# Decode attention with a gate: K turned in 32x32 blocks on VectorE, block-diagonal queries, longer K/V chunks and a ring of 3

## The chip, the cores and the metric

The kernel runs on one core of one Trainium2 chip. The metric is the device time of one execution in microseconds; less is better. All times are medians of several executions. PE is TensorE, PEld its weight loads, DVE is VectorE, ACT is ScalarE, POOL is GpSimd, SP is the queue that issues the large loads. The "span" is the time of the profiled execution on the core; it is about 2 us less than the device time.

## The reference, cut to what matters

```
q = (x @ wq) -> 16 heads of 256          # one token
k_cache, v_cache: [8 groups, 65536 keys, 256] bf16     # 2 heads share a group
p = softmax(q . k / 16);  o = p . v;  a = o @ wo       # 448 outputs
b = small MLP on layernorm(x)
out = g * a + (1 - g) * b,  g = sigmoid(sum(x * gate_w))
```

K and V are 2 x 268 MB, and each element is used for two heads only. The kernel has to read 537 MB and does little with them.

## The kernel before

K and V of one group come in chunks of 64 rows per partition: 32 KB per partition, 4 MB per load. Each chunk is 4 steps of 16 rows per partition. Loads go into a ring of 5 slots, K and V in turn. The matmul needs K with the head dimension on the partitions, so K is turned. Before the change PE turns it (16 transposes per step, two bf16 values taken as one fp32), and DVE copies the result from PSUM:

```python
NB = 64; SB = 16; STEPS = NB // SB; RING = 5; LAG = 4
...
def transposes(n, half):
    ...
    for jj in range(8):
        nc.tensor.transpose(tp[:, 128 * jj:128 * jj + 128], kn[:, j0 + jj, :], ident[:])
    nc.vector.tensor_copy(
        out=kT[n % 2][:, 8 * DH * half:8 * DH * (half + 1)], in_=tp[:].bitcast(BF16)
    )

def scores(n):               # four column groups of PE side by side, 8 matmuls of 512 columns
    for c in range(2):
        for a in range(4):
            nc.tensor.matmul(sc[n % 2][32 * a:32 * a + 32, :], lhsT=qT[:, c, g]..., 
                rhs=kv[:, :, 32 * a:32 * a + 32, c], ..., tile_position=(0, 32 * a))
    nc.scalar.activation(out=p_t[n % 2][:], in_=sc[n % 2][:], func=ACT.Exp, ...)

def p_transpose(n):
    nc.vector.transpose(out=pT_t[n % NPT][:], in_=p_t[n % 2][:])
# p_v(n - LAG): 8 matmuls with V;  per step 32 matmuls and 32 weight loads on PE
# at the end of a group: o_scale (DVE), o_turn (PE), o_out (PE)
```

The softmax here doesn't subtract the row's maximum and nothing guards it: scores larger than these inputs give would overflow.

## Time and profile before

Time before: 1289.4 us, median of 3 runs (1289.29 to 1289.5).

| of the span of 1287.6 us | value | view |
|---|---|---|
| PE busy | 74% | busy table |
| DVE busy | 62% | busy table |
| DMA, 20 to 1250 us | share 1.00, about 430 GB/s | table by stretches |
| period of one K and V pair | 19.66 us | landings in the chain of waits |
| last V rows in, end of the span | 1279.9 us, 1287.6 us | DMA packets in the trace, page |

First, lines of the page of the kernel before: the slices (share of the DMA engines in tenths, and their rate), the DMA queues with packets, MB and share, and the chain that ended last by engine.

```profile
DMA  9999999999999999999999999999999999999995
GB/s 392 431 430 433 427 432 425 429 432 429 433 425 433 429 431 428 429 430 429 432 429 426 433 430 430 430 430 427 435 427 433 425 430 431 430 430 418 436 421 241
...
q1 hardware_dynamic: 19730, 540.55, 98.0%
...
q8 instruction: 66, 1.08, 0.3%
...
DMA 62%; PE 37%; DVE 1%; issue 0%; ACT 0%; SPq 0%; ACTq 0%; DVEq 0%
```

The DMA is full in every slice but the last. Queue 8 has 66 packets of 16 KB. The trace has 8454 matmuls and 8454 weight loads; 66 times 256 is 16,896, so these are PE's instructions, 256 to a packet (16,908 were recorded).

Second, the table by stretches of the kernel before: stretch and its length, busy time of the engines (instructions), granted PE clock, DMA share, GB/s.

```profile
1200.00:1240.00 40.00, 30.96 (x274) 19.02 (x273) 25.51 (x27) 5.56 (x17) 0.00 (x0) 0.87 1.00 428
...
1260.00:1270.00 10.00, 10.00 (x103) 6.42 (x103) 9.45 (x10) 2.67 (x8) 0.00 (x0) 1.00 0.96 396
1270.00:1275.00 5.00, 5.00 (x56) 3.04 (x57) 4.63 (x6) 0.74 (x3) 0.00 (x0) 1.00 0.57 236
1275.00:1280.00 5.00, 3.62 (x49) 1.55 (x48) 3.99 (x6) 1.38 (x4) 0.00 (x0) 1.00 0.37 145
```

Third, groups of instructions before: line, engine, operation, output and input with shapes, count, busy us and mean ns, and the idle time before them.

```profile
L316 DVE COPY kT_141<-tps_75 128x2048 bf16<-128x2048 bf16 x128 | 156.4, 1222 | 95.2 <-PE tps_75 L315 94.8
L337 DVE STREAM_TRANSPOSE pT_145<-p_143 128x512 bf16<-128x512 bf16 x43 | 30.2, 701 | 0.0
```

### The profile page before, as it was taken

The page shows a single profiled execution, that of the slowest core. Times are in us where ns is not written, and L with a number is a line of the kernel's source. Part 1 is how long each engine was busy: PE and PEld are TensorE (multiplying, and loading weights), DVE is VectorE, ACT ScalarE, POOL GpSimd, SP SyncE. Part 2 cuts the span into 40 slices and gives each one's busy share as a digit, 9 for nine tenths or more (in the row PEclk, how much of TensorE's full clock was granted, in tenths as well). Part 3 has the DMA queues.
Part 4 walks back from the last instruction along what each step waited for, and adds up shares of the span by engine and source line. Part 5 has one row for each costly group of instructions (what it writes and reads, how often), then busy time and mean ns, then how long its engine had stood idle before and what let it go on. Part 6 is the DMA issues. An engine that isn't in the chain of part 4 may idle for free.

```text
span 1287.6 us, 19500 instructions
## 1 busy us (share of the span) xinstructions
PE 952.5 (74%) x8454; PEld 595.9 (46%) x8454; DVE 792.6 (62%) x859; ACT 193.2 (15%) x543; POOL 80.2 (6%) x101
## 2 busy tenths in 40 slices
PE   4586777876877767778768677696786876877878
PEld 3354444544544444445445444454454544544544
DVE  3565755756666557566566575674665755656657
ACT  0111111211111111111111111111111111111111
POOL 2110111100111001110000000000000000000000
PEclk9887888888888788788888897887887888889889
DMA  9999999999999999999999999999999999999995
GB/s 392 431 430 433 427 432 425 429 432 429 433 425 433 429 431 428 429 430 429 432 429 426 433 430 430 430 430 427 435 427 433 425 430 431 430 430 418 436 421 241
DMA packets 21196, 545.49 MB, mean 424 GB/s; under 512 B 2675, under 2 KB 2806, under 8 KB 3958
## 3 DMA queue, kind: packets, MB, share of 16 engines
q1 hardware_dynamic: 19730, 540.55, 98.0%
q0 software_dynamic: 1376, 3.69, 0.8%
q8 instruction: 66, 1.08, 0.3%
q14 instruction: 20, 0.16, 0.0%
q10 hardware_dynamic: 4, 0.00, 0.0%
HBM read 544.22 MB, written 0.00 MB: 423 GB/s over the span
## 4 chain that ended last, share of the span: by engine, by line
DMA 62%; PE 37%; DVE 1%; issue 0%; ACT 0%; SPq 0%; ACTq 0%; DVEq 0%
DMA ring_73<-in_A_k_cache_dram 15%; PE tps_74 L315 12%; DMA ring_69<-in_A_k_cache_dram 12%; DMA ring_72<-in_A_k_cache_dram 12%; PE tps_75 L315 12%; DMA ring_71<-in_A_k_cache_dram 12%; DMA ring_70<-in_A_k_cache_dram 11%; PE pv L347 6%; PE sc_77 L325 4%; PE sc_76 L325 3%; DMA ring_73<-in_A_wq_dram 1%; PE misc L292 0%; PE misc L247 0%; DVE kT_142 L316 0%; PE misc L357 0%
## 5 line engine op out<-in xcount | busy, mean ns | idle before, releaser
L316 DVE COPY kT_141<-tps_74 128x2048 bf16<-128x2048 bf16 x128 | 154.8, 1209 | 350.5 <-PE tps_74 L315 350.5
L316 DVE COPY kT_141<-tps_75 128x2048 bf16<-128x2048 bf16 x128 | 156.4, 1222 | 95.2 <-PE tps_75 L315 94.8
L331 ACT ACTIVATE p_144<-sc_77 128x512 bf16<-128x512 f32 x128 | 76.4, 597 | 710.0 <-PE sc_77 L325 710.0
L316 DVE COPY kT_142<-tps_75 128x2048 bf16<-128x2048 bf16 x128 | 156.7, 1224 | 25.2 <-PE tps_75 L315 24.6
L316 DVE COPY kT_142<-tps_74 128x2048 bf16<-128x2048 bf16 x128 | 152.7, 1193 | 7.8 <-PE tps_74 L315 7.3
L331 ACT ACTIVATE p_143<-sc_76 128x512 bf16<-128x512 f32 x128 | 76.4, 597 | 368.8 <-PE sc_76 L325 368.8
L315 PE MATMUL tps_74<-ident,ring_69 128*128 128x128 f32 x416 | 68.7, 318 | 66.6 <-DMA ring_69<-in_A_k_cache_dram 66.5
L315 PE MATMUL tps_74<-ident,ring_71 128*128 128x128 f32 x416 | 68.8, 319 | 65.5 <-DMA ring_71<-in_A_k_cache_dram 65.5
L315 PE MATMUL tps_74<-ident,ring_70 128*128 128x128 f32 x416 | 66.0, 310 | 63.5 <-DMA ring_70<-in_A_k_cache_dram 63.5
L315 PE MATMUL tps_74<-ident,ring_73 128*128 128x128 f32 x416 | 67.0, 313 | 58.5 <-DMA ring_73<-in_A_k_cache_dram 58.0
L315 PE MATMUL tps_74<-ident,ring_72 128*128 128x128 f32 x384 | 62.3, 315 | 63.8 <-DMA ring_72<-in_A_k_cache_dram 63.8
L325 PE MATMUL sc_77<-kT_142,qT 128*32 128x512 bf16 x1024 | 105.0, 495 | 1.2 <-DVE kT_142 L316 1.2
L315 PEld LDWEIGHTS tps_74<-ident,ring_71 128*128 128x128 f32 x416 | 54.6, 163 | 91.5 <-issue 89.4
L315 PEld LDWEIGHTS tps_74<-ident,ring_69 128*128 128x128 f32 x416 | 54.8, 163 | 89.6 <-issue 88.0
L315 PEld LDWEIGHTS tps_74<-ident,ring_70 128*128 128x128 f32 x416 | 52.3, 158 | 86.6 <-issue 84.9
L315 PEld LDWEIGHTS tps_74<-ident,ring_73 128*128 128x128 f32 x416 | 53.1, 160 | 82.4 <-issue 77.6
L315 PEld LDWEIGHTS tps_74<-ident,ring_72 128*128 128x128 f32 x384 | 49.3, 161 | 85.3 <-issue 83.6
L325 PE MATMUL sc_76<-kT_141,qT 128*32 128x512 bf16 x1024 | 79.3, 385 | 0.2
L315 PE MATMUL tps_75<-ident,ring_69 128*128 128x128 f32 x416 | 67.8, 316 | 0.0
L315 PE MATMUL tps_75<-ident,ring_71 128*128 128x128 f32 x416 | 66.7, 312 | 0.0
L315 PEld LDWEIGHTS tps_75<-ident,ring_69 128*128 128x128 f32 x416 | 53.8, 161 | 26.9 <-issue 26.9
L315 PEld LDWEIGHTS tps_75<-ident,ring_71 128*128 128x128 f32 x416 | 52.8, 159 | 27.6 <-issue 27.6
(133 smaller groups left out, 976.5 us busy)
## 6 DMA issues: line engine op xcount, KB each, us to landing
ring_69<-in_A_k_cache_dram SPq DMA_DIRECT2D x13, 4096.0 KB, 25.1
ring_70<-in_A_v_cache_dram SPq DMA_DIRECT2D x13, 4096.0 KB, 34.5
ring_71<-in_A_k_cache_dram SPq DMA_DIRECT2D x13, 4096.0 KB, 24.8
ring_72<-in_A_v_cache_dram SPq DMA_DIRECT2D x13, 4096.0 KB, 34.2
ring_73<-in_A_k_cache_dram SPq DMA_DIRECT2D x13, 4096.0 KB, 24.5
ring_69<-in_A_v_cache_dram SPq DMA_DIRECT2D x13, 4096.0 KB, 33.9
ring_70<-in_A_k_cache_dram SPq DMA_DIRECT2D x12, 4096.0 KB, 24.2
ring_71<-in_A_v_cache_dram SPq DMA_DIRECT2D x12, 4096.0 KB, 33.6
```

What stands on the lines that cost most here:

```text
L315: nc.tensor.transpose(tp[:, 128 * jj:128 * jj + 128], kn[:, j0 + jj, :], ident[:])
L316: nc.vector.tensor_copy(out=kT[n % 2][:, 8 * DH * half:8 * DH * (half + 1)], in_=tp[:].bitcast(BF16))
L325: nc.tensor.matmul(sc[n % 2][32 * a:32 * a + 32, :], lhsT=qT[:, c, g].rearrange("p r x -> p (r x)"), rhs=kv[:, :, 32 * a:32 * a + 32, c], ...
L331: nc.scalar.activation(out=p_t[n % 2][:], in_=sc[n % 2][:], func=ACT.Exp, scale=scale, accum_out=den[g % 2][:, n % steps_g:n % steps_g + 1],)
L347: nc.tensor.matmul(pv[32 * a:32 * a + 4, :], lhsT=pT[:, i, :, 0], rhs=vt[:, j * DH:(j + 2) * DH], start=first and i < 4, stop=last and i > ...
```

## The change

The intent is to take the turning of K off PE, to halve PE's instructions, to have one softmax per chunk instead of one per step, and to make rows longer. DVE turns K in 32x32 blocks. A 32x32 transpose does not gather a whole head dimension, so the queries are laid out block-diagonally: with 8 full-width matmuls per step, a window that slides by one column per step puts each step's scores on other rows of one PSUM tile. The chunks are of 6, 6, 5, 5, 5 and 5 steps (48 or 40 KB per partition) in a ring of 3. The diff, cut to its core:

```diff
-NB = 64
-STEPS = NB // SB
-RING = 5
-LAG = 4
+SIZES = (6, 6, 5, 5, 5, 5)
+RING = 3
+PAD = MAXS - 1
+WIN = 128 + PAD
...
-    def transposes(n, half):
-        ... 16 PE transposes per step, 2 copies from PSUM
+    def turn(i, s, n):
+        kn = ring[2 * i % RING][:].bitcast(FP32)
+        nc.vector.transpose(
+            out=kT[n % 2][:].bitcast(FP32), in_=kn[:, s * SB * 128:(s + 1) * SB * 128]
+        )
...
+        for q in range(8):
+            nc.tensor.matmul(
+                sc[i % 2][:], lhsT=qw[g % 2][:, q, PAD - s:PAD - s + 128], rhs=kv[:, :, q // 2, :, q % 2],
+                start=(s == 0 and q == 0), stop=(s == sizes[c] - 1 and q == 7),
+            )
...
+    for i in range(total):          # per chunk: all turns and scores, one softmax, all P V
+        for s in range(sizes[c]):
+            turn(i, s, n); scores(i, s, n); ...
+        load(2 * i + RING)
+        softmax(i)
+        for s in range(sizes[c]): p_v(i, s)
+        load(2 * i + 1 + RING)
```

## The prediction

> **What bounds the kernel now: the DMA engines, not compute.** The page's slices show DMA 9 in every slice but the last, at 425 to 433 GB/s. The Trainium skill ("DMA: Bandwidth & Descriptors", "Where 436 GB/s comes from") puts the ceiling of the ports at 435.2 GB/s; this trace comes within 1.5%. The table by stretches shows a DMA share of 1.00 from 20 to 1250 us. The chain of waits is 62% DMA: each pair of K and V takes 19.66 us (landings at 539.1, 578.5 and 617.8 us for every second pair), and PE works about 15 us of it, then idles 4 to 6 us. Loads are issued some 5 us before the one ahead lands (24 us from issue to landing, 19.7 us per pair), so the queue never runs dry. PE 74%, DVE 62% are not binding. Only the end is serial: the last data lands near 1279.8, the end is 1287.6; 6 us of it is normalise, turn, project.
>
> **What the change removes.** 16 fp32 PE transposes per step (2.05 us warm for 16) and two PSUM copies (1.2 us each); the exp and the P transpose per step (0.6 + 0.19 and 0.70 us) become one per chunk. All off the critical path.
>
> **What it adds.** One VectorE block transpose per step, 128x2048 fp32. The bf16 one of 128x512 takes 701 ns, about 0.17 us plus one column per cycle. The skill's "Vector Engine (DVE) Microarchitecture Reference" (3.8) says one element per cycle per lane, and this trace agrees for bf16; no 4-byte one is here. Estimate 2.3 us per step, 590 us in all. Scores become 8 full-width 512-column matmuls one after another instead of four column groups side by side (0.55 us for 8, so about 0.27 us each): about 2.1 us per step, 550 us. Estimates: DVE about 640 us (50%), PE about 700 us (55%). A 6-step chunk needs about 14 us of turning and 18 us to its softmax, against 29.5 us in which its 48 KB of K and of V arrive. With three slots, V of the next chunk is issued some 15 us after K lands, K after that at about 22 us; each time one load is still whole in the queue. The DMA stays saturated: the ring of 3 costs nothing in the steady part.
>
> **What moves the time.**
> 1. Rows of 40 or 48 KB instead of 32 KB. In the trace's packets 32 KB took 1215 ns and 8 KB 311 ns: 9.7 ns fixed per packet. A quarter of the packets go: about -2.5 us.
> 2. Half of PE's instructions go; each 16 KB instruction fetch lengthened one neighbouring K/V packet by about 0.5 us, on one of some eight engines in turn (66 fetches): about -2 us.
> 3. The end: V is ready earlier, no PE backlog: about -1 us.
> 4. The last K's pieces are issued only after the K before it is turned (5 steps, about 12.7 us with a cold PE), while the one load in flight lasts 12.3 us: a hole of about 1.5 us: +1.5 us.
>
> Sum: about -4 us: **1285 us, range 1277 to 1292.** Faster by over 2%: 0.02; within 2%: 0.94; slower: 0.04.
>
> **Signs.** Right: DMA still 9 in all slices and about 430 GB/s; block transposes near 2.3 us; PE and DVE shares falling to 50 to 60%; DMA over 60% of the chain. A hole in DMA near 1240 to 1260 us shows point 4.
>
> **What would make it wrong.** The 4-byte transpose taking two cycles per element (4.5 us): a 6-step chunk then takes 27 us of 29.5, slots come free too late, and the time could pass 1300. Long rows split into smaller packets: no gain in 1. Full-array matmuls throttled to half speed (3.4 us per step) would lengthen the hole.

## The result, and the profile after

After the change: 1283.0 us (1281.83 to 1283.69, 4 runs), against 1289.35 us before (4 runs). The ratio is 0.995, 95% interval 0.9933 to 0.9967. Ratios are the mean time of one kernel's runs over that of the other's of the same rounds, so not quite the ratio of the medians quoted. The forecast of 1285 us and its range held, in part by luck. As the terms below show, the fetch term was too small by 3.5 to 4.2 us and a hole of 1.5 us did not come; the end term, wrong in its sign, and the row term together took back 2.0 to 2.7 us of that.

The same lines of the page as before, for the kernel after:

```profile
DMA  9999999999999999999999999999999999999996
GB/s 395 435 426 431 434 434 431 425 433 434 430 422 434 430 429 432 424 431 432 430 436 414 432 437 434 427 421 430 435 429 438 419 430 429 436 430 419 439 420 288
...
q1 hardware_dynamic: 15410, 540.55, 98.4%
...
q8 instruction: 34, 0.56, 0.2%
...
DMA 56%; PE 24%; DVE 14%; issue 6%; ACT 1%; DVEq 0%; SPq 0%
```

It is still a kernel bound by DMA. PE has fallen to 60% and DVE to 51%, as expected; that this alone is worth nothing is shown by the run e9 below. The instruction packets went from 66 to 34.

The groups that cost most after the change:

```profile
L351 DVE STREAM_TRANSPOSE kT_265<-ring_71 128x2048 f32<-128x2048 f32 x48 | 110.2, 2295 | 74.8 <-DMA ring_71<-in_A_k_cache_dram 63.3
...
L359 PE MATMUL sc_72<-kT_265,qw_283 128*128 128x512 bf16 x288 | 93.6, 481 | 113.7 <-DVE kT_265 L351 113.7
```

The block transpose of 128x2048 fp32 takes 2295 ns, as estimated. The trace after also has one of 128x128 fp32, with 311 ns. The two give 1.03 ns per column and 0.18 us fixed, and with these a transpose of 512 columns should take 0.71 us; the bf16 ones took 711 ns. So 4-byte elements go at the same rate per column as 2-byte ones. The trace of before has one size only and could not show this split.

The end of the table by stretches, after:

```profile
1240.00:1250.00 10.00, 9.06 (x32) 3.42 (x31) 7.45 (x4) 0.00 (x0) 0.00 (x0) 0.81 0.96 406
1250.00:1260.00 10.00, 7.98 (x65) 3.11 (x64) 7.99 (x5) 0.69 (x2) 0.00 (x0) 1.00 1.01 422
1260.00:1270.00 10.00, 6.08 (x38) 2.68 (x40) 4.96 (x7) 0.69 (x2) 0.00 (x0) 1.00 1.00 413
1270.00:1281.00 11.00, 5.71 (x48) 2.62 (x40) 1.52 (x4) 0.00 (x0) 0.00 (x0) 0.71 0.07 28
```

Here the DMA stays full to 1270 us and then stops at once. There is no stretch at 0.57 any more. That difference made me look at the 16 DMA engines one by one. (The stretch as such is not the gain. With the ring of 3 it is absent also in e2 below, which gains nothing.) A load's completion semaphore gets one increment from each engine (the Trainium skill, "DMA: Bandwidth & Descriptors", "Why a DMA increments its semaphore by 16 and not by 1", says that they "finish independently"). This trace agrees: the increments of one load lie apart, and I sorted them. The columns are the 16 engines in order of finishing, in us behind the first:

```
before, load landing at   55 us: 0.0 0.1 0.1 0.2 0.2 0.3 0.3 0.3 0.4 0.7 0.7 0.8 1.1 1.1 1.7 2.0
before, load landing at  549 us: 0.0 0.3 0.7 0.7 0.8 0.9 1.7 3.6 4.4 4.4 4.5 5.0 5.1 5.9 6.1 6.2
before, load landing at 1142 us: 0.0 0.3 0.5 0.5 0.6 0.7 3.8 8.6 10.6 10.6 10.7 10.8 11.1 11.3 12.1 12.4
before, load landing at 1275 us: 0.0 0.6 0.6 0.7 0.8 1.6 1.6 7.3 9.9 10.1 10.2 10.2 10.3 10.6 10.9 11.6
after,  last K/V piece         : 0.0 0.1 0.2 0.3 0.3 0.4 0.5 0.7 0.9 1.2 1.3 1.3 1.7 1.8 2.2 2.7
```

Before the change the engines drift apart over the run, about 1 us in 100 us, and about half of them are late. All engines carry the same bytes of K and V, and a load is complete only when the slowest engine is. So the late engines set the time at which each load is complete; that they set the time of the kernel is tested by the runs below. In the traces the last V rows landed at 1279.9 us before and 1272.5 us after: 7.4 us of the gain lie before that point. After that point, 0.5 us were lost (7.7 us to the end before, 8.2 us after).

One thing more bears on the end of before. The chain that ended last there is work of PE from 1249.9 us on, when the K before the last one landed: PE had a backlog, and the last V rows came in just before it was through. So the last V rows alone did not set that end. What the backlog cost can be estimated from e8 below, which has none and ends 6.8 us after its last rows, against 7.7 us here: about 1 us.

### The profile page after: what moved, and what is told of

Read it like the earlier page. It is cut to its first block, busy times and chain, and to the rows that moved or that the text cites. A ratio compares the mean times of both kernels' runs of the same rounds, so it can differ in the third digit from the quotient of the medians.

```text
span 1280.7 us, 10114 instructions
## 1 busy us (share of the span) xinstructions
PE 763.0 (60%) x4390; PEld 293.5 (23%) x4390; DVE 647.5 (51%) x423; ACT 51.0 (4%) x127; POOL 88.7 (7%) x147
## 4 chain that ended last, share of the span: by engine, by line
DMA 56%; PE 24%; DVE 14%; issue 6%; ACT 1%; DVEq 0%; SPq 0%
DMA ring_69<-in_A_k_cache_dram 21%; DMA ring_70<-in_A_k_cache_dram 17%; PE sc_72 L359 17%; DMA ring_71<-in_A_k_cache_dram 16%; DVE kT_265 L351 8%; DVE kT_266 L351 4%; PE pv_74 L381 2%; PE pv_75 L381 2%; DMA ring_71<-in_A_v_cache_dram 1%; DVE pT_269 L370 1%; PE sc_73 L359 1%; PE misc L414 1%; PE misc L424 1%; ACT p_267 L366 1%; DVE acc L429 0%
## 5 line engine op out<-in xcount | busy, mean ns | idle before, releaser
L359 PEld LDWEIGHTS <-qw_282 128*128 128x128 bf16 x1024 | 111.1, 110 | 397.3 <-issue 174.4
L359 PEld LDWEIGHTS <-qw_283 128*128 128x128 bf16 x1024 | 110.4, 110 | 390.3 <-issue 154.6
L359 PE MATMUL sc_72<-kT_265,qw_283 128*128 128x512 bf16 x288 | 93.6, 481 | 113.7 <-DVE kT_265 L351 113.7
L359 PE MATMUL sc_72<-kT_265,qw_282 128*128 128x512 bf16 x288 | 94.0, 482 | 108.1 <-DVE kT_265 L351 108.1
L351 DVE STREAM_TRANSPOSE kT_265<-ring_71 128x2048 f32<-128x2048 f32 x48 | 110.2, 2295 | 74.8 <-DMA ring_71<-in_A_k_cache_dram 63.3
L351 DVE STREAM_TRANSPOSE kT_266<-ring_69 128x2048 f32<-128x2048 f32 x48 | 109.8, 2288 | 71.3 <-DMA ring_69<-in_A_k_cache_dram 63.6
L351 DVE STREAM_TRANSPOSE kT_265<-ring_70 128x2048 f32<-128x2048 f32 x40 | 91.6, 2289 | 81.0 <-DMA ring_70<-in_A_k_cache_dram 70.3
L351 DVE STREAM_TRANSPOSE kT_265<-ring_69 128x2048 f32<-128x2048 f32 x40 | 92.0, 2300 | 61.5 <-DMA ring_69<-in_A_k_cache_dram 44.3
L351 DVE STREAM_TRANSPOSE kT_266<-ring_70 128x2048 f32<-128x2048 f32 x40 | 91.7, 2291 | 60.2 <-DMA ring_70<-in_A_k_cache_dram 47.9
L359 PE MATMUL sc_73<-kT_266,qw_282 128*128 128x512 bf16 x288 | 83.7, 440 | 60.6 <-DVE kT_266 L351 60.2
L359 PE MATMUL sc_73<-kT_266,qw_283 128*128 128x512 bf16 x288 | 81.7, 432 | 60.1 <-DVE kT_266 L351 60.1
L351 DVE STREAM_TRANSPOSE kT_266<-ring_71 128x2048 f32<-128x2048 f32 x40 | 90.9, 2273 | 1.5 <-PE sc_72 L359 1.4
L359 PE MATMUL sc_73<-kT_265,qw_282 128*128 128x512 bf16 x224 | 61.8, 422 | 31.5 <-DVE kT_265 L351 31.4
L359 PE MATMUL sc_72<-kT_266,qw_283 128*128 128x512 bf16 x224 | 67.7, 454 | 15.6 <-DVE kT_266 L351 15.6
L359 PE MATMUL sc_72<-kT_266,qw_282 128*128 128x512 bf16 x224 | 66.1, 445 | 13.6 <-DVE kT_266 L351 13.6
L359 PE MATMUL sc_73<-kT_265,qw_283 128*128 128x512 bf16 x224 | 60.4, 415 | 17.9 <-DVE kT_265 L351 17.8
L370 DVE STREAM_TRANSPOSE pT_269<-p_267 128x512 bf16<-128x512 bf16 x24 | 17.1, 711 | 67.5 <-ACT p_267 L366 67.5
L370 DVE STREAM_TRANSPOSE pT_270<-p_268 128x512 bf16<-128x512 bf16 x24 | 17.1, 711 | 67.3 <-ACT p_268 L366 67.3
L381 PEld LDWEIGHTS <-pT_269 128*4 128x4 bf16 x1024 | 23.4, 89 | 77.0 <-DVE pT_269 L370 49.7
L366 ACT ACTIVATE p_267<-sc_72 128x512 bf16<-128x512 f32 x24 | 14.3, 597 | 657.8 <-PE sc_72 L359 657.8
L381 PEld LDWEIGHTS <-pT_270 128*4 128x4 bf16 x1024 | 24.2, 91 | 63.1 <-DVE pT_270 L370 32.3
L366 ACT ACTIVATE p_268<-sc_73 128x512 bf16<-128x512 f32 x24 | 14.3, 597 | 526.5 <-PE sc_73 L359 526.5
```

The costliest lines, as they stand in the source:

```text
L351: nc.vector.transpose(out=kT[n % 2][:].bitcast(FP32), in_=kn[:, s * SB * 128:(s + 1) * SB * 128])
L359: nc.tensor.matmul(sc[i % 2][:], lhsT=qw[g % 2][:, q, PAD - s:PAD - s + 128], rhs=kv[:, :, q // 2, :, q % 2], start=(s == 0 and q == 0), s ...
L366: nc.scalar.activation(out=p_t[i % 2][:], in_=sc[i % 2][:], func=ACT.Exp, scale=scale, accum_out=den[g % 2][:, c:c + 1],)
L370: nc.vector.transpose(out=pT_t[i % 2][:], in_=p_t[i % 2][:])
L381: nc.tensor.matmul(pv[g % 2][32 * a:32 * a + 4, :], lhsT=pT[:, k, :, s], rhs=vt[:, j * DH:(j + 2) * DH], start=first and k < 4, stop=last ...
```

## What the late engines do: theory and rivals

In the trace of before I looked at the 46 instruction packets between 300 and 1200 us. Each starts 3 ns before a K/V packet ends, takes 1066 ns on the mean, and the K/V packet that follows, which starts some 15 ns before the fetch ends, takes 499 ns longer than the usual 1215 ns. So a fetch holds its engine up for 1.55 us. The lengths of the fetches repeat with a period of eight (1018, 1074, 1069, 1061, 1107, 1100, 1088, 1016, 1026, 1073 ns ...), which suggests that they go to eight engines in turn. The trace doesn't name the engine of a packet; that eight engines are late is shown below. The Trainium skill ("Runtime: NRT & Kernel Launch", "Instruction fetch mechanics") says that each engine's instructions come in 16 KB blocks of 256 over a DMA queue, and that the cost of crossing from one block to the next is "mostly hidden". The size agrees with these traces. Whether PE waits for a fetch was not examined; the DMA engine loses 1.55 us to each, and K and V wait there.

- Theory A: each fetch costs its engine about 1.5 us; eight engines share the fetches, and the slowest sets the pace. Then 32 fetches fewer are 4 per engine, or about -6 us.
- Theory B: the fetches count by their bytes only, spread over all engines: about -1.2 us.
- Theory C: the gain comes from less work on PE and DVE, or from the end, and not from fetches.
- Rival for the rest: the gain is in the longer rows, not in the arithmetic.

## The experiments

Twelve kernels were run, all correct, in three batches. Beside them the kernel before took 1289.49, 1289.43 and 1289.30 us. "Last rows" below is the time in the profiled span at which the last rows of V had landed.

| run | edit of the kernel after | us | 16 KB fetches | last rows | end of span |
|---|---|---|---|---|---|
| e0_after | none | 1283.41 | 34 | 1273.3 | 1282.2 |
| e2_split | matmuls cut in two | 1289.00 | 66 | 1279.5 | 1289.6 |
| e1_rows32_ring5 | 32 KB rows, ring of 5 | 1282.75 | 34 | 1274.3 | 1281.3 |
| e3_rows16_ring8 | 16 KB rows, ring of 8 | 1298.26 | 34 | 1283.7 | 1296.2 |
| e9_split_rows32_ring5 | both of e2 and e1 | 1289.00 | 66 | 1279.8 | 1288.5 |
| e10_split4_rows32_ring5 | e1, scores cut in four | 1294.01 | 82 | 1283.2 | 1290.4 |
| e7_rows32_ring3 | 32 KB rows, ring of 3 | 1301.38 | 34 | 1291.3 | 1298.4 |
| e4_korder | K first at the end | 1283.58 | 34 | 1272.3 | 1280.9 |
| e5_warm | idle matmuls at the end | 1288.02 | 34 | 1271.7 | 1285.6 |
| e6_order_warm | e4 and e5 | 1286.34 | 34 | 1272.2 | 1280.9 |
| e8_order_light | e4, few idle matmuls | 1280.94 | 34 | 1272.3 | 1279.0 |
| e11_order_light_rows32 | e8 and e1 | 1282.96 | 34 | 1274.3 | 1281.2 |

### The reference

> The kernel after the change, unaltered, as the reference for the runs beside it. All theories: 1283 us, within 1.5 us, 34 instruction packets of 16 KB on queue 8, last V rows landing near 1272.5 us of the span.

It took 1283.41 us (1281.96 to 1284.23), with a spread of over 2 us where the kernel before mostly has a few tenths. In the profile the last P V took 4.4 us here, where 40 such matmuls take 2.3 us in the first profile of the same kernel; turning and projecting, 1.65 us each there, took 1.05 and 0.92 us here. The end of this kernel varies, as will be seen.

### As many instructions as before

```diff
-            nc.tensor.matmul(sc[i % 2][:], lhsT=qw[...], rhs=kv[:, :, q // 2, :, q % 2], ...)
+            for u in range(2):
+                nc.tensor.matmul(sc[i % 2][:, 256 * u:256 * u + 256], lhsT=qw[...],
+                                 rhs=kv[:, 8 * u:8 * u + 8, q // 2, :, q % 2], ...)
 # and P V cut into two of 256 columns in the same way
```

> The kernel after the change, with every score and every P V matmul cut into two of 256 columns: the same data and the same reads, but PE again has about as many instructions as before the change (34 fetches of 16 KB become about 66). Theory A (each fetch costs its own DMA engine 1.5 us: 1.05 us of its own and 0.49 us added to the next packet; fetches go to about half of the 16 engines; the slowest engine sets the pace): 4 more fetches on each of the slow engines, +5 to +6 us, 1288 to 1289 us. Theory B (only the bytes count, 0.52 MB over 16 engines at 430 GB/s): +1.2 us, 1284 us. Theory C (the gain came from the engines' work at the end and not from fetches): no change, 1283 us.

It took 1289.00 us, ratio to before 0.9994 (0.9982 to 1.0007). The whole gain is gone, although nothing was changed but the number of PE instructions (matmuls and weight loads, of which each matmul has one). PE was busy 60% as without the cut. B and C expected 1284 and 1283 us and fall. The DMA share near the end does not show the loss here: it is still 1.00 from 1270 to 1275 us, since with the ring of 3 all 16 engines finish within 3.7 us of each other.

### Rows and ring of before

```diff
-SIZES = (6, 6, 5, 5, 5, 5)
-RING = 3
+SIZES = (4,) * 8
+RING = 5
```

> The kernel after the change with the loads of before: eight chunks of 4 steps, 32 KB rows, a ring of 5. Row theory (9.7 ns fixed per packet): a third more packets than with 40 and 48 KB rows, +2.5 us, 1285.5 us, packets of 32 KB at 1215 ns. Rival, that the long rows and the ring of 3 are worth nothing and all comes from the compute side: 1283 us. Rival, that the gain is all in the rows: 1289 us.

It took 1282.75 us (1282.56 to 1283.08), no slower than the kernel after. Taken alone, this says that long rows are worth nothing. The last rows landed at 1274.3 us, 1.0 to 1.8 us later than in the two profiles of the kernel after, but the end took 7.0 us against 8.2 and 8.9. So a part is gained by the rows and lost again at the end; e8 and e11 below separate the two.

### Short rows

```diff
-SIZES = (6, 6, 5, 5, 5, 5)
-RING = 3
+SIZES = (2,) * 16
+RING = 8
-    wq_slot = ring[RING - 1]
+    wq_slot = ringp.tile([128, 14336], BF16, name="wq_slot")
```

> The kernel after the change with sixteen chunks of 2 steps, 16 KB rows, a ring of 8, and the query weights in a tile of their own. Row theory: 2.7 times the packets of 40 and 48 KB rows, 9.7 ns fixed each, +12 us, 1295 us. If short rows cost nothing: 1283 us.

It took 1298.26 us. The last rows landed 9.4 us after those of e1. By the fixed 9.7 ns per packet, 16 KB rows have 1024 packets more per engine than 32 KB rows, or 9.9 us, so the packet term holds. The packets took 613 ns, which also agrees with 9.7 ns plus the rate. The other 6 us are at the end: with chunks of 2 steps, the last K piece lands only 2 us before the last V rows, and 12.5 us pass from there to the end.

### Cut in two, and in four, with the loads of before

> The kernel after the change with the loads of before (32 KB rows, ring of 5) and every score and P V matmul cut in two, so that PE has as many instructions as before the change (66 fetches of 16 KB instead of 34). The loads and the fetches are then those of before; only the arithmetic is that of after. Fetch theory, 1.5 us of its engine for each fetch, four more on each of the slow engines: 1282.75 + 6 = 1289 us, with the DMA engines drifting some 12 us apart by the end. If the change of arithmetic is worth something by itself: 1283 to 1285 us.

> As the run with 32 KB rows and a ring of 5, with every score matmul cut in four of 128 columns and P V left whole: some 82 fetches of 16 KB, 48 more than without the cut, six more on each of eight engines. Fetch theory: 1282.75 + 9 = 1292 us, DMA engines 16 to 18 us apart by the end. If PE becomes the limit instead (32 weight loads and matmuls per step), PE is busy over 90% and the DMA share falls below 1.

The second of them cuts each score matmul into four of 128 columns and leaves P V whole. These three lines are from the pages of e1, e9 and e10, in that order (packets, MB, share):

```profile
q8 instruction: 34, 0.56, 0.2%
```

```profile
q8 instruction: 66, 1.08, 0.3%
```

```profile
q8 instruction: 82, 1.34, 0.4%
```

And these are the 16 engines in the last pieces of K and V, sorted, us behind the first:

```
e1,  34 fetches: 0.0 0.3 0.5 0.8 0.9 1.3 1.5 4.7 6.2 6.2 6.3 6.4 6.4 6.8 7.9 8.5
e9,  66 fetches: 0.0 0.2 0.2 0.3 0.8 1.4 1.4 4.6 12.1 12.2 12.3 12.3 12.6 12.8 12.9 13.9
e10, 82 fetches: 0.0 0.1 0.2 0.4 0.9 1.1 1.2 4.5 15.1 15.1 15.1 15.3 15.3 15.4 16.0 16.8
```

Eight engines are late, and they are later the more fetches there are. (A ninth is late by 4.5 to 4.7 us in all three, whatever the fetches; why is not known.) The last rows landed at 1274.3, 1279.8 and 1283.2 us: 5.5 us for 4 more fetches on each of eight engines, 8.9 us for 6 more. That is 1.4 to 1.5 us per fetch. The medians are 1282.75, 1289.00 and 1294.01 us; the last is 2 us above the expected 1292 us, with a spread of 1291.8 to 1296.4 us whose profile (span 1290.4 us) does not show why. PE was busy 59 to 60% in all three, and a count of the DMA packets finds no engine idle between 40 and 1225 us in any of them, so PE did not hold up the loads. And e9, which has before's loads and before's number of fetches but the arithmetic of after, takes before's time: ratio 0.9996 (0.9983 to 1.0008). So beyond its fewer instructions the new arithmetic shows no gain that these runs could see.

### A ring of 3 with 32 KB rows

```diff
-SIZES = (6, 6, 5, 5, 5, 5)
+SIZES = (4,) * 8
```

> The kernel after the change with 32 KB rows (eight chunks of 4 steps) and the ring left at 3: against the run with a ring of 5, 1282.75 us, this takes away queued loads alone. If a ring of 3 costs nothing because the slow DMA engines never run dry: 1283 to 1284 us, with more idle time of the fast DMA engines. If 4-step chunks leave a ring of 3 too short (a first chunk of a group takes about 19 us of the 19.7 us per pair): several us more, up to 1300 us, with gaps in all DMA engines at the group starts. I lean to the first for seven of eight chunks and to a few us of loss at group starts: 1285 us.

It took 1301.38 us, 18.6 us more than with a ring of 5. I leaned to 1285 us and missed. A line of its table by stretches shows the loss, though it looks small there:

```profile
800.00:1200.00 400.00, 239.76 (x1330) 90.12 (x1322) 200.98 (x124) 13.76 (x40) 1.50 (x2) 0.83 0.99 422
```

The DMA share is 0.99 and the rate 422 GB/s, where the other kernels have 427 to 430. Counting in the DMA packets how many of the 16 engines were at work, about 17 us per engine were idle between 40 and 1225 us; with a ring of 5 it was at most 0.3 us. So the ring of 3 costs little only together with the longer chunks.

The kernel after itself is near this edge. This is its timeline at the first chunk of a group, with a 48 KB chunk in ring_69 (start, length, instruction, idle time before it):

```profile
500.46 2.31 DVE L351 STREAM_TRANSPOSE kT_265<-ring_69 128x2048 f32<-128x2048 f32 x1 [6.58 <-DMA ring_69<-in_A_k_cache_dram]
502.83 3.59 PE L359 MATMUL sc_72<-kT_265,qw_283 128*128 128x512 bf16 x8 [10.10 <-DVE kT_265 L351]
...
524.54 2.31 DVE L351 STREAM_TRANSPOSE kT_266<-ring_69 128x2048 f32<-128x2048 f32 x1 [0.40 <-PE sc_72 L359]
526.88 0.33 SPq L87 DMA_DIRECT2D ring_69<-in_A_v_cache_dram  x1
...
531.17 2.31 DVE L351 STREAM_TRANSPOSE kT_265<-ring_71 128x2048 f32<-128x2048 f32 x1 [0.89 <-DMA ring_71<-in_A_k_cache_dram]
```

The first scores take 3.59 us for 8 matmuls, against 1.90 us when PE has been busy for a while. With those, and the work of the group before in between, six turns take 26.4 us instead of the 14 us that I had put. The next V is asked for at 526.9 us, only about 4 us before the load in flight lands. Between 40 and 1225 us the engines were idle for about 1 and 2 us per engine in the two profiles of this kernel, in short stretches at the group starts: the engines that are ahead wait there for the late ones. That fits the spread, which stays small after the change (2.7 and 4.0 us) while it grows to 8.5 us in e1, which has the same fetches and a deeper ring. Whether the late engines lose a little there as well is not settled: e2, with the long rows and the ring of 3, landed its last rows no earlier than e9 with short rows and the ring of 5 (1279.5 and 1279.8 us), so 2 us of the rows' gain may have been lost to the ring at 66 fetches.

### The end

At the end of the kernel after, the last K piece comes after the first V piece, and PE no longer has its full rate. The Trainium skill ("TensorE: Matmul & The Clock Gate", "What's actually happening") puts an idle PE at half the clock. The traces agree: 8 score matmuls took 3.59 us after a wait and 1.90 us later, and the granted clock is 0.71 in the last stretch above. These are the last pieces in the trace after: P V with the last rows, scaling, turning and projecting.

```profile
1273.05 0.39 PE L381 MATMUL pv_75<-ring_71,pT_270 128*4 128x512 bf16 x3 [0.36 <-DMA ring_71<-in_A_v_cache_dram]
1273.49 0.75 DVE L405 TENSOR_SCALAR pvs<-pv_75,rden 128x512 f32<-128x512 f32 x1 [3.48 <-PE pv_75 L381]
1274.29 1.64 PE L414 MATMUL misc<-sel,pvs 128*128 128x2 f32 x8 [0.85 <-DVE pvs L405]
1275.97 0.16 DVE L418 CAST oT<-misc 128x4 bf16<-128x4 f32 x1 [1.73 <-PE misc L414]
1276.19 1.65 PE L424 MATMUL misc<-wo_94,oT 128*1 128x448 bf16 x4 [0.25 <-DVE oT L418]
```

In the kernel before, PE had worked without a pause from 1250 to 1277 us, and the two PE pieces of this chain took 1.07 and 0.93 us. These are lines of its chain of waits (start, length, work):

```profile
1226.33 23.41 DMA ring_73<-in_A_k_cache_dram
1249.87 1.94 PE tps_74 L315 x8
...
1282.36 1.07 PE misc L373 x8
...
1283.67 0.93 PE misc L383 x4
```

So in this profile the change gave back 1.3 us. Five runs try to take that away.

```diff
 # e4_korder: the last K piece before the first V piece
-            piece(item, 0, SB)
             piece(item - 1, (last - 1) * SB, SB)
+            piece(item, 0, SB)
 # e5_warm: matmuls of a constant into a spare PSUM bank
+        if i == total - 1: warm(7)          # before P V of the last chunk
+                if i == total - 1: warm(4)  # after P V of each of its steps but the last
+    warm(3)                                 # before the last o_turn
 # e6_order_warm: both
```

> The kernel after the change, with the last 8 KB piece of K asked for before the first piece of V at the end, so that all of K is in 2.4 us earlier. In two profiles of the kernel after the change, the span ends 8.2 and 8.9 us after the last V rows land, with P V of the last chunk (40 matmuls, 2.3 us warm and 4.4 us cold) partly or wholly after them. If the end is held by the chain behind the last K piece: -0.5 to -2.5 us, 1281 to 1282.5 us. If only the last V rows hold it: no change.

> The kernel after the change, with some 30 idle matmuls of 512 columns put into the waits of the last chunk and the last output projection, to keep PE at its full rate there. If the cold PE costs at the end (o_turn and o_out 1.65 us each against 1.0, P V 4.4 against 2.3): -1 to -2 us, 1281.5 to 1282.5 us. If not: no change, or +0.5 us from the idle matmuls.

> Both of the edits of the end together (K pieces first, PE kept warm): -2 to -3 us, about 1280.5 us, with the span ending 6.5 us after the last V rows land. If the fetches alone set the time, 1283 us.

e4 took 1283.58 us: no gain. P V no longer ran late (it ended 1.1 us after the last rows), but turning and projecting took 1.87 and 1.65 us. e5 took 1288.02 us and e6 1286.34 us, both worse. The fillers themselves were in the way: in e5, P V was late anyway, its last step stood behind 23 idle matmuls in PE's order, and it ended at 1279.7 us, 8 us after the last rows. In e6 it ended 2.8 us after them, in a profile of one of its two shorter runs (1282.8 us; the three longer ones took 1286.3 to 1287.4 us and were not profiled). But turning and projecting took 1.05 and 0.92 us in both, so the rate was the right thing to work on.

```diff
 # e8_order_light: e4, and fillers only where PE waits for V
+                if i == total - 1 and s >= sizes[c] - 3:
+                    warm(5 if s == sizes[c] - 3 else 2)
+    warm(3)
 # e11_order_light_rows32: the same with SIZES = (4,) * 8 and RING = 5
```

> The kernel after the change, with the last K piece before the first V piece, and idle matmuls only where PE waits for V at the very end (5 before the wait for the fourth V piece, 2 before the fifth, 3 while the sums are scaled). The run with fillers everywhere was held by its own fillers: P V ended 2.8 us or more after the last rows. Here P V should end 0.6 us after the last rows and o_turn and o_out take 1.0 us each: -1.5 us against the kernel after the change, about 1281.7 us.

> The same edits of the end on 32 KB rows and a ring of 5 (1282.75 us without them). -1 to -1.5 us: about 1281.5 us. If longer rows are worth the 2.5 us of the prediction, this is slower than the run with 40 and 48 KB rows and the same end; if they are worth nothing, the two are equal.

e8 took 1280.94 us (1280.75 to 1283.53), ratio to before 0.9937 (0.9924 to 0.9949). Its median is below those of both kernels, by 2.5 us for e0_after, though that ran in another batch, one of the five runs took 1283.53 us, and the two ratios to before (0.9937 and 0.9949) have intervals that overlap. So a gain of 1.5 to 2.5 us over the kernel after is likely, not certain. Its last pieces, with PE at its full rate:

```profile
1272.74 0.39 PE L382 MATMUL pv<-ring,pT 128*4 128x512 bf16 x3 [0.37 <-DMA ring<-in_A_v_cache_dram]
...
1273.98 1.05 PE L415 MATMUL misc<-sel,pvs 128*128 128x2 f32 x8
...
1275.28 0.92 PE L425 MATMUL misc<-wo,oT 128*1 128x448 bf16 x4 [0.25 <-DVE oT L419]
```

e11 took 1282.96 us, 0.2 us more than e1: its end was not cold in e1 (1.05 and 1.06 us), and there was nothing to win. With the same end, 40 and 48 KB rows in a ring of 3 are 2.0 us better than 32 KB rows in a ring of 5 (1280.94 and 1282.96 us; 1.4 us between the means), and the last rows land 2.0 us earlier (1272.3 and 1274.3 us). The six profiles with the long rows and 34 fetches all have the last rows at 1271.7 to 1273.3 us, the two with 32 KB rows and a ring of 5 at 1274.3 us. This answers what e1 left open: the rows are worth nearly what was predicted, and the cold end hid it.

## Why the prediction was right or wrong

| term | predicted | measured | from |
|---|---|---|---|
| 1. longer rows | -2.5 us | -2.0 us | e8 against e11, same end (with the ring of 3 in it) |
| 2. fewer instruction fetches | -2 us | -5.5 us in the last rows, -6.2 us in the medians | e1 against e9 |
| 3. the end | -1 us | +0.5 to +1.2 us | last rows to end, 7.7 us before, 8.2 and 8.9 after |
| 4. a hole before the last K | +1.5 us | 0 | trace of after |
| sum | -4 us | -6.4 us | 1289.35 and 1283.0 us |

The frame was right: DMA bound before and after, near 430 GB/s, PE and DVE off the critical path, the 4-byte transpose at 2.3 us. DMA has 56% of the chain instead of over 60%.

Term 2 failed in its size. The step was "each 16 KB instruction fetch lengthened one neighbouring K/V packet by about 0.5 us, on one of some eight engines in turn". Eight engines in turn was right, and so was the 0.5 us. But I counted only the neighbour and not the 1.07 us of the fetch packet itself, in which that engine moves no K or V. Together it is 1.55 us in the trace, and 1.4 to 1.5 us in the runs with 34, 66 and 82 fetches. The lateness of some engines was to be seen in the profile of before: a share of 0.57 in the stretch from 1270 to 1275 us.

Term 3 failed in its sign. "V is ready earlier, no PE backlog" overlooked that an idle PE is slow: without the backlog, turning and projecting took 1.65 us each instead of about 1.0 in the first profile, and in that of e0 P V took 4.4 us instead of 2.3. Without that cost the term holds: e8, whose PE is kept warm, ends 6.8 us after its last rows, against 7.7 us before the change.

Term 4 failed as a mechanism. "The last K's pieces are issued only after the K before it is turned" took the order of the program for the order of waiting. The loads have a queue of their own and wait for their slot, not for the instructions written before them. SP's queue in the trace after shows it:

```profile
1225.25 0.33 SPq L87 DMA_DIRECT2D ring_69<-in_A_v_cache_dram  x1
1229.36 1.82 SPq L87 DMA_DIRECT2D ring_70<-in_A_k_cache_dram  x4
1238.46 0.33 SPq L87 DMA_DIRECT2D ring_71<-in_A_v_cache_dram  x1
```

Four of the five last K pieces (ring_70) go out at 1229.4 us, when P V of two chunks earlier frees the slot; the K before it is turned from 1236 us on. The fifth goes out at 1238.8 us, behind a V piece whose place that turning frees. The DMA share stays at 0.96 to 1.01 there, and no DMA engine is idle from 1225 to 1265 us.

"The ring of 3 costs nothing in the steady part" was true by a small margin only. The 15 us to the issue of the next V were 26.4 us at group starts, and with 32 KB rows the same ring cost 18.6 us.

## What to carry to other kernels

When DMA is full, ask what each DMA engine carries besides the data: in these runs the engines that also fetched instructions finished last and set the time, so halving the instructions of an engine that isn't the bottleneck can still be worth more than longer rows. Sum such a cost on the engine that carries most of it, with the whole time that it takes from the data, and look for a fall of the DMA share to about one half at the end as its sign. A deep ring is needed for that sign: with a ring of 5 and 66 fetches the engines ended 11.6 to 13.9 us apart, with a ring of 3 only 3.7 us, at the same loss. Freeing PE also let it go cold just before the serial end; a few idle matmuls in its real waits probably paid there, but many of them in front of work that was ready cost several us.

## What the Trainium skill lacked or had wrong

- "Runtime: NRT & Kernel Launch", "Instruction fetch mechanics", calls the cost of crossing a 16 KB boundary "mostly hidden". In this kernel, bound by DMA, it isn't: a block took 1.55 us from its DMA engine in the trace, and 32 blocks fewer were worth 5.5 us in the last rows' landing (1279.8 and 1274.3 us) and 6.2 us in the median time.
- No page has that PE's blocks delay only eight of the 16 DMA engines (eight are late at 34, 66 and 82 blocks, and the fetch lengths repeat with a period of eight), or that the last of these then finishes up to 16.8 us after the first engine (82 blocks).
- "DMA: Bandwidth & Descriptors", "Queues, rings and completion order", puts the refill on row 14. In these traces PE's 16 KB blocks are on queue 8 (66 before, 34 after), and queue 14 has the 20 and 10 other instruction packets, if the profile's queue numbers are that page's rows, which no run shows.
- The same page ("Measured (HBM→SBUF, 128 partitions, SWDGE, issued from GpSimd)") gives a time per packet for small packets only, about 10.5 ns in a transfer of 4 KB. In these traces a row of 8, 16, 32, 40 and 48 KB took 311, 613, 1215, 1516 and 1818 ns, so about 10 ns are fixed per row, and going from 16 to 32 KB rows was worth 9.4 us of 1284.
- No page has a 4-byte block transpose on DVE: 128x2048 fp32 took 2295 ns and 128x128 fp32 311 ns, 1.03 ns per column as with bf16. That fits the one element per cycle per lane of "Vector Engine (DVE) Microarchitecture Reference" (3.8), though no run shows the length of a cycle.
